# Two decode layers on one core: layer 0's feed-forward in one part, small w2 products in 512 columns, a 24 KB ring and 4 KB more of K kept

## The chip, the cores and the metric

The kernel runs on one core of one Trainium2 chip. The metric is the device time of one execution in microseconds (us); three runs of the kernel before gave 705.28 us in the median, 705.11 at the least and 705.5 at the most. Sizes such as "4 KB" are bytes per partition throughout; a load of 4 KB fills 128 partitions and moves 512 KB.

## What is computed

Two transformer layers, one token for each of four sequences, float32. Both layers use the same weights and the same caches.

```
x = A_x                                      # 4 x 1 x 512
for layer in range(2):
    h = layernorm(x)                         # no gain, no bias
    q = (h @ wq) as 32 heads of 128          # wq 512 x 4096
    p = softmax(q . k_cache / sqrt(128))     # k_cache 4 x 8 x 4096 x 128, four heads share one
    x = x + (p . v_cache) @ wo               # v_cache as k_cache, wo 4096 x 512
    h = layernorm(x)
    x = x + (silu(h @ w1) * (h @ w3)) @ w2   # w1, w3 512 x 1792, w2 1792 x 512
```

The caches hold 64 MiB each and are read once in each layer, apart from what stays on the chip between the layers.

## The kernel before

SBUF is one tile, `arena`, of 218 KB per partition, and the program manages it by hand. A plan (the list `plan`, lines 89 to 160) names every load in order: source, size, the keys under which its parts are used, and, where it matters, a fixed address. `pump` (L164) issues the next loads of the plan on SyncE's queue for as long as `take` (L56) finds room. It is called from `done` (L195) and `vacate` (L203), when the last reader of a load has been issued; the load that takes the room then waits on the chip for those readers. So the order of the loads is fixed, and what paces them is the room.

Each of 8 KV heads has 64 KB of K and 64 KB of V. Scores (L400 to L421) run over 8 blocks of 512 keys, each with four products of 512 columns, one for each sequence, in four column groups of TensorE. Layer 0 takes the heads in rising order, layer 1 in falling order, so that head 7 (`TURN`) is last in the one and first in the other. Between the layers all of wq (64 KB at 0), wo (64 KB at 64) and V of head 7 (64 KB at 128, `KEPT`) stay in `arena`. The first block of head 7's K is partly kept too: layer 0 copies its first 2 KB into PSUM (`keptk`, L417) and the next 2 KB into `first` at the end of `arena` (L418), and layer 1 begins with these (L405 to L408) in place of the first of eight half blocks of 4 KB.

What is left, 28 KB, is the **ring** (L124 to L143): seven slots of 4 KB, six from address 192 on and one at 64, where the first 4 KB of wo lay until they were moved to PSUM (`stash`, L498). Through these slots pass, in the order of the plan, layer 0's w1 and w3 and w2 and then seven half blocks of head 7's K for layer 1. Behind them come blocks 4 to 7 of that K in loads of 8 KB, which take the room that wq's groups leave as layer 1's q products are done (`q_product`, L348).

The feed-forward (L521 to L617) has two parts. The 1792 hidden columns lie as four groups of 448, in four column groups of TensorE; the first part takes 256 of each group's columns, the second the other 192. For layer 0 the pieces are: w1 first part, four of 4 KB; w3 first part, four of 4 KB; w1 second part, four of 3 KB; w3 second part, four of 3 KB; w2, seven of 4 KB, two of its 14 row tiles each. After each piece `busy` (L288) adds products of no use that fill TensorE's time in layer 0. `gate`, `join` and the transposes of the first part run between the products of the second. In layer 1 (not in the ring) the last loads of the program are w1 and w3 of the first part (16 KB each), of the second (12 KB each), and w2 in loads of 8, 8, 4, 4 and 2 KB for row tiles 1 to 13. Row tile 0 of w2 is loaded ahead in another layout (`w2s`): eight tiles of 16 rows in 16 partitions. Each of these and each later row tile is multiplied by `columns` (L554): four products of 128 columns, one for each column group, into `x_ps`. Then 128 columns of `x_ps` are copied and stored.

```
def columns(rows, m, w, last=False):
    for k in range(KC):
        nc.tensor.matmul(x_ps[32 * k:32 * k + B, 0:P], hT[rows, m, :], w[rows, k * P:(k + 1) * P],
                         start=False, stop=last)
```

Of the kernel before, what the change touches and what calls it, by code (L numbers as in the profile page):

```python
# [9 lines left out]
AF = mybir.ActivationFunctionType  # L10
# [13 lines left out]
FA = 2 * P  # L24
FB = FJ - FA
WT = 14
FEW = 16
EPS = 1e-5
SCALE = DH ** -0.5
# [6 lines left out]


@with_exitstack
def tile_decode_layers(ctx: ExitStack, tc: tile.TileContext, x, kt, v, wq, wo, w1, w3, w2, w2s, out):
# [59 lines left out]
    def weights(name, src, layer, parts, per, at=None, first=0):  # L99
        r = 0  # L100
        for n in parts:
            load(src[:, r * KB:(r + n) * KB], per, [(name, layer, first + r // per + j) for j in range(n // per)],
                 None if at is None else at + r)
            r += n

# [10 lines left out]

    def piece(name, i, at):

        w, layer, lo, n, per = {"w1a": (w1, 0, 4 * i, 4, 4), "w3a": (w3, 0, 4 * i, 4, 4),
                                "w1b": (w1, 0, 16 + 3 * i, 3, 3), "w3b": (w3, 0, 16 + 3 * i, 3, 3),  # L120
                                "w2": (w2, 0, 4 * i, 4, 2), "half": (kt[TURN], 1, 4 * i, 4, 4)}[name]
        weights(name, w[:, lo * KB:(lo + n) * KB], layer, (n,), per, at, 2 * i if name == "w2" else i)

    RING = KEPT + 64  # L124
    slots = [WO] + [RING + 4 * i for i in (5, 4, 3, 2, 1, 0)]
    for i in range(4):
        piece("w1a", i, (slots[6], slots[1], slots[2], slots[3])[i])
    for i in range(4):
        piece("w3a", i, (slots[4], slots[5], slots[0], slots[6])[i])
    for i in range(4):  # L130
        piece("w1b", i, RING + 21 - 3 * i)
    for i in range(2):
        piece("w3b", i, RING + 9 - 3 * i)
    piece("w2", 0, slots[0])
    for i in range(2, 4):
        piece("w3b", i, RING + 9 - 3 * i)
    for i in range(1, 7):
        piece("w2", i, slots[i])
    for i in range(7):
        piece("half", i + 1, slots[i])  # L140
    ring["to"] = len(plan) - 1
    cache("k", 1, TURN, (8,) * (NB - SPLIT), SPLIT)
    for n in range(1, HKV):  # L143
# [9 lines left out]
        plan.append((*next(side), "few", None))  # L153

    for part, per, at in (("a", 4, 0), ("b", 3, 16)):
        for name, w in (("w1", w1), ("w3", w3)):
# [7 lines left out]
    def pump():  # L164
        while state["next"] < len(plan):
            src, per, keys, at = plan[state["next"]]
            n = src.shape[-1] // KB
# [12 lines left out]
            if a is None:  # L180
                return
            nc.sync.dma_start(arena[:, a * KB:(a + n) * KB], src)
            i = state["next"]
            if i == 0:
                nc.sync.dma_start(xt[:8], x[:8])
            left[i] = (len(keys), a, n)
            for j, key in enumerate(keys):
                where[key] = (a + j * per, per, i)
            state["next"] += 1

    def loaded(*key):
        a, n, _ = where[key]
        return arena[:, a * KB:(a + n) * KB]

    def done(*key):  # L195
        i = where[key][2]
# [73 lines left out]
    nc.vector.memset(x_ps, 0.0)  # L270

    first = arena[:, FIRST * KB:]
    pT = arena[:, PT * KB:FIRST * KB].rearrange("p (i r) -> p i r", i=NI)

    def small(name, n=1, bufs=1):
# [245 lines left out]
    def feed_forward(layer, mean):  # L521
        keep = layer < LAYERS - 1
        h = p[:, 0:FJ]

        def product(name, ps, lo, n, fill=(0, 0, 0, 0), ks=range(KC)):
            for k in ks:
                w = loaded(name, layer, k)
                for j in range(4):
                    nc.tensor.matmul(ps[32 * j:32 * j + 32, lo:lo + n], x32[:, k, :], w[:, j * n:(j + 1) * n],  # L529
                                     start=(k == 0), stop=(k == KC - 1))  # L530
                done(name, layer, k)
                busy(fill[k] if keep else 0)

        def gate(lo, n):
            a = h[:, lo:lo + n]
# [15 lines left out]
                done("w2", layer, 2 * i + n)  # L551
            busy((1, 2, 2, 2, 1, 2, 0)[i])

        def columns(rows, m, w, last=False):  # L554
            for k in range(KC):
                nc.tensor.matmul(x_ps[32 * k:32 * k + B, 0:P], hT[rows, m, :], w[rows, k * P:(k + 1) * P],  # L556
                                 start=False, stop=last)

        def few(lo, hi):
            for u in range(lo, hi):  # L560
                at = (where["few"] + 2 * u) * KB
                columns(slice(0, FEW), WT + u, arena[:, at:at + 2 * KB])

        sq = squares()
        product("w1a", s_ps, 0, FA, (0, 0, 2, 0))
        rstd = deviation(sq, total(flat(sq)))
        mean()
        if not keep:
            nc.vector.tensor_tensor(xt, xc, mu.unsqueeze(1).broadcast_to([P, KC, B]), op=ALU.add)
        product("w3a", o_ps, 0, FA, (2, 2, 2, 2))  # L570
        if not keep:
            for k in range(KC):
                nc.tensor.matmul(x_ps[32 * k:32 * k + B, 0:P], xt[:, k, :], ident, start=True, stop=False)
            busy(4)
        gate(0, FA)
        join(0, FA)
        product("w1b", s_ps, FA, FB, (1, 1, 1, 1))
        if keep:
            gate(FA, FB)
            nc.scalar.activation(spare, half, AF.Exp)  # L580
        for i in range(2):
            nc.tensor.transpose(t_ps[:, i, :], h[:, i * P:(i + 1) * P], ident)
        if not keep:
            for u in range(8):
                nc.tensor.matmul(t_ps[0:FEW, 2, B * u:B * u + B], h[0:32, FEW * u:FEW * u + FEW], ident[0:32, 0:B],
                                 start=True, stop=True)
            busy()
        tiles(0, 8)
        if not keep:
            nc.vector.tensor_copy(hT[0:FEW, WT:WT + 8, :], t_ps[0:FEW, 2, 0:8 * B].rearrange("p (u b) -> p u b", b=B))  # L590
            gate(FA, FB)
            few(0, 4)
        product("w3b", o_ps, FA, FB, (1, 2, 1, 1), range(0, 2))
        if keep:
            down(0)
        product("w3b", o_ps, FA, FB, (1, 2, 1, 1), range(2, KC))
        join(FA, FB)

        def tail_tiles():
            nc.tensor.transpose(t_ps[:, 2, :], h[:, FA:FA + P], ident)  # L600
            for u in (0, 64):
                nc.tensor.matmul(t_ps[u:u + 64, 3, 0:64], h[u:u + 64, FA + P:FJ], ident[u:u + 64, u:u + 64],
                                 start=True, stop=True)
            tiles(8, 6)

        if keep:
            for i in range(1, WT // 2):
                if i == 4:
                    tail_tiles()
                down(i)  # L610
            return
        few(4, 8)
# [98 lines left out]
```

## Time and profile before

| | before |
|---|---|
| median of 3 runs | 705.28 us |
| the profiled execution | 705.23 us |
| its span, first to last instruction | 703.4 us |
| TensorE matmul busy | 409.9 us (58%) |
| VectorE busy | 85.2 us (12%) |
| ScalarE busy | 38.0 us (5%) |
| GpSimd busy | 3.5 us |
| bytes moved by DMA | 298.85 MB, mean 425 GB/s |
| granted TensorE clock, mean | 0.808 |

The span is what lies between the first and the last instruction; the rest of the profiled execution's time, 1.8 us, lies around it. The DMA share is the mean busy share of the core's 16 DMA engines. It is worked out from the packets' recorded times, so it can go a little above 1 in a short stretch. A granted clock of 1 is 2.4 GHz, and 0.5 is 1.2 GHz.

### The profile page before, as it was taken

To read this page: it belongs to the slowest core of one execution; us is meant where nothing else is said; L and a number is where in the kernel's file an instruction comes from. 1 tells how busy PE (TensorE), PEld (TensorE's weight loads), DVE (VectorE), ACT (ScalarE), POOL (GpSimd) and SP (SyncE) were. 2 spreads that over 40 slices of the span, in tenths; PEclk is the share of its full clock that TensorE was granted. 3 is DMA by queue.
4 is the path that set the end of the run, shared out by engine and by line. 5 is a ranking of instruction groups with operands and counts; after the bars stand their busy time and mean duration, and the time that the engine had idled before them with its cause. 6 is when DMAs were issued, how large, how long until landed. Compare 5 with 4: busy or idle time off the path is not lost. (4 is left out here: it accounts for less than half of the span.)

```text
span 703.4 us, 7079 instructions
## 1 busy us (share of the span) xinstructions
PE 409.9 (58%) x3172; PEld 136.4 (19%) x3172; DVE 85.2 (12%) x291; ACT 38.0 (5%) x87; POOL 3.5 (0%) x11
## 2 busy tenths in 40 slices
PE   2555454456456454538888894365563545467687
PEld 1112011112111111112233331011120111122234
DVE  2001010101001010101111111020000101010111
ACT  0000000000000000101001000000000000000100
POOL 0000000000000000000000000000000000000000
PEclk9986776767777776878999997588787878688899
DMA  9999999999999999999999999999999999999996
GB/s 418 432 403 466 422 418 426 462 415 432 433 444 418 440 444 421 421 428 427 414 404 403 420 431 461 429 425 418 459 425 425 437 444 418 432 433 420 424 424 277
DMA packets 13605, 298.85 MB, mean 425 GB/s; under 512 B 1655, under 2 KB 1783, under 8 KB 6263
## 3 DMA queue, kind: packets, MB, share of 16 engines
q1 hardware_dynamic: 13440, 298.39, 99.1%
q8 instruction: 25, 0.41, 0.2%
q14 instruction: 5, 0.04, 0.0%
q10 hardware_dynamic: 135, 0.01, 0.0%
HBM read 298.33 MB, written 0.07 MB: 424 GB/s over the span
## 5 line engine op out<-in xcount | busy, mean ns | idle before, releaser
L461 PE MATMUL o_ps<-arena 128*32 128x512 f32 x1024 | 146.8, 723 | 144.4 <-DMA arena<-in_v 131.0
L414 PE MATMUL s_ps<-arena,qpad 128*32 128x512 f32 x1020 | 150.1, 742 | 90.1 <-DMA arena<-in_kt 90.1
L461 PEld LDWEIGHTS o_ps<-arena 128*32 128x32 f32 x1024 | 37.4, 130 | 251.9 <-issue 222.4
L414 PEld LDWEIGHTS s_ps<-arena,qpad 128*32 128x32 f32 x1020 | 39.5, 132 | 183.7 <-issue 176.6
L470 DVE SCALAR_TENSOR_TENSOR p<-o_ps,parts,p 128x512 f32<-128x512 f32 x16 | 12.0, 751 | 266.9 <-PE o_ps L461 266.9
L424 DVE TENSOR_REDUCE top<-s_ps 128x1 f32<-128x512 f32 x16 | 11.1, 691 | 196.9 <-PE s_ps L414 196.9
L468 ACT ACTIVATE p<-o_ps,parts 128x512 f32<-128x512 f32 x16 | 11.0, 687 | 189.9 <-PE o_ps L461 182.3
L292 PE MATMUL m_ps<-ident,rows 128*32 128x256 f32 (+1 forms) x84 | 20.9, 352 | 0.0
L352 PE MATMUL o_ps<-arena,xpad 128*32 128x512 f32 x112 | 15.4, 672 | 7.9 <-DMA arena<-in_wq 7.9
L447 PE MATMUL t_ps<-ident,p 128*128 128x128 f32 x64 | 11.4, 305 | 13.5 <-ACT p L441 13.5
L474 PE MATMUL t_ps<-ident,p 128*128 128x128 f32 x64 | 10.5, 287 | 13.9 <-DVE p L470 13.8
L496 PE MATMUL x_ps<-arena,qT 128*4 128x512 f32 x112 | 13.8, 592 | 5.4 <-DVE qT L482 3.6
L434 ACT ACTIVATE f<-d 128x1 f32<-128x1 f32 x16 | 3.2, 203 | 252.8 <-DVE d L432 252.8
L441 ACT ACTIVATE p<-s_ps,top 128x512 f32<-128x512 f32 x16 | 10.9, 684 | 77.3 <-PE t_ps L474 77.3
L448 DVE COPY arena<-t_ps 128x512 f32<-128x512 f32 x16 | 11.1, 691 | 9.7 <-PE t_ps L447 9.7
L474 PEld LDWEIGHTS t_ps<-ident,p 128*128 128x128 f32 x64 | 6.7, 140 | 28.2 <-DVE p L470 28.2
L447 PEld LDWEIGHTS t_ps<-ident,p 128*128 128x128 f32 x64 | 7.3, 150 | 22.2 <-ACT p L441 19.2
L292 PEld LDWEIGHTS m_ps<-ident,rows 128*32 128x32 f32 x84 | 9.0, 110 | 9.0 <-issue 3.5
L529 PE MATMUL o_ps<-arena,xpad 128*32 128x192 f32 (+1 forms) x128 | 8.1, 360 | 1.0 <-DMA arena<-in_w 0.9
L529 PE MATMUL s_ps<-arena,xpad 128*32 128x192 f32 (+1 forms) x128 | 7.9, 359 | 1.3 <-DMA arena<-in_w 1.3
L489 PE MATMUL x_ps<-arena,qT 128*4 128x256 f32 x88 | 6.6, 379 | 2.4 <-DMA arena<-in_w 1.7
L352 PEld LDWEIGHTS o_ps<-arena,xpad 128*32 128x32 f32 x112 | 3.6, 121 | 17.2 <-DMA arena<-in_wq 8.8
(107 smaller groups left out, 144.2 us busy)
## 6 DMA issues: line engine op xcount, KB each, us to landing
arena<-in_v SPq DMA_DIRECT2D x4, 4096.0 KB, 38.4
arena<-in_w SPq DMA_DIRECT2D x17, 512.0 KB, 13.4
arena<-in_kt SPq DMA_DIRECT2D x8, 1024.0 KB, 11.3
arena<-in_kt SPq DMA_DIRECT2D x2, 4096.0 KB, 18.1
arena<-in_wq SPq DMA_DIRECT2D x1, 7168.0 KB, 39.8
arena<-in_v SPq DMA_DIRECT2D x3, 2048.0 KB, 31.8
arena<-in_wo SPq DMA_DIRECT2D x1, 4096.0 KB
arena<-in_kt SPq DMA_DIRECT2D x2, 2048.0 KB
```

The source lines that it names most:

```text
L292: nc.tensor.matmul(m_ps[0:32, (4 - w) * P:], rows, ident.unsqueeze(1).broadcast_to([P, w, P]), start=True, stop=True)
L352: nc.tensor.matmul(ps[32 * k:32 * k + 32, :], xpad[:, 32 * k + lo:32 * k + lo + 32], w[:, k, :], start=first, stop=last)
L414: nc.tensor.matmul(s_ps[32 * b:32 * b + 32, :], qpad[:, 32 * b + lo:32 * b + lo + 32], k[:, j, :], start=(blk == 0), stop=(blk == NB - 1))
L424: nc.vector.tensor_reduce(top[:, 0:1], s_ps, axis=AX.X, op=ALU.max, negate=True)
L447: nc.tensor.transpose(t_ps[:, i, :], p[:, i * P:(i + 1) * P], ident)
L448: nc.vector.tensor_copy(pT.rearrange("p i r -> p (i r)"), t_ps.rearrange("p i r -> p (i r)"))
L461: nc.tensor.matmul(o_ps[32 * b:32 * b + 32, :], pT[:, i, 32 * b:32 * b + 32], w[:, b, :], start=(i == 0), stop=(i == NI - 1))
L468: nc.scalar.activation(p, o_ps, AF.Copy, scale=st["parts"][:, 0:1])
L470: nc.vector.scalar_tensor_tensor(p, o_ps, st["parts"][:, 1:2], p, op0=ALU.mult, op1=ALU.add)
L474: nc.tensor.transpose(t_ps[:, j, :], p[:, j * P:(j + 1) * P], ident)
L496: nc.tensor.matmul(x_ps[r:r + B, :], left(2 * i + n), w(n), start=first, stop=False)
L529: nc.tensor.matmul(ps[32 * j:32 * j + 32, lo:lo + n], x32[:, k, :], w[:, j * n:(j + 1) * n], start=(k == 0), stop=(k == KC - 1))
```

## The change

Layer 0's feed-forward runs in one part: all of w1 in eight pieces of 3.5 KB (one piece is two column groups of 448 columns for one of the four row blocks), then all of w3 in eight such pieces, then `join`, the transposes and w2. The filling products after each piece of w1 and w3 are gone; those after w2's pieces stay, and four units stand behind w3. Layer 1 keeps the two parts (sources `w1l`, `w3l`, laid out as before).

The ring has six slots (24 KB): five from 196 on and the one at 64. The 4 KB at 192 (`MORE`) are kept out of the free room from the start; layer 0 copies the second half of the first block of head 7's K there (GpSimd, 1024 elements), and layer 1 uses it and then gives the room back. So six half blocks are loaded in place of seven.

In layer 1, the eight tiles of 16 rows and row tiles 1 to 4 of w2 are multiplied by `wide`: one product of 512 columns for each, into `s_ps`, four in turn in the four column groups. Then `s_ps` is copied to SBUF and added to `x_ps` by four products of 128 columns. Row tiles 5 to 13 stay with `columns`.

```
+WIDE = 5
+HALF = 2 * FJ / 256
-    PT, FIRST = ARENA - 4, ARENA - 2
-    free = [(WO, PT - WO)]
+    PT, FIRST, MORE = ARENA - 4, ARENA - 2, KEPT + 64
+    free = [(WO, MORE - WO), (MORE + 4, PT - MORE - 4)]
...
-    RING = KEPT + 64
-    slots = [WO] + [RING + 4 * i for i in (5, 4, 3, 2, 1, 0)]
...
-    for i in range(7):
-        piece("half", i + 1, slots[i])
+    RING = MORE + 4
+    slots = [WO] + [RING + 4 * i for i in (4, 3, 2, 1, 0)]
+    small_loads = [(name, i) for name, n in (("w1", 2 * KC), ("w3", 2 * KC), ("w2", WT // 2)) for i in range(n)]
+    small_loads += [("half", i) for i in range(2, 2 * SPLIT)]
+    for n, (name, i) in enumerate(small_loads):
+        piece(name, i, slots[(5, 1, 2, 3, 4, 0)[n % 6]])
...
-                for b, k in enumerate((p, first)):
+                for b, k in enumerate((p, first, more_k[:, 0:BK], more_k[:, BK:])):
...
-                del keys[0]
+                give(MORE, 4)
+                pump()
+                keys = []
...
                 nc.gpsimd.tensor_copy(first, loaded(*keys[0])[:, BK:2 * BK])
+                nc.gpsimd.tensor_copy(more_k, loaded(*keys[0])[:, 2 * BK:])
...
         if keep:
-            for i in range(1, WT // 2):
...
+            product("w1", s_ps)
+            rstd = deviation(sq, total(flat(sq)))
+            mean()
+            gate(0, FJ)
+            nc.scalar.activation(spare, half, AF.Exp)
+            product("w3", o_ps)
+            join(0, FJ)
+            busy(4)
+            for i in range(2):
+                nc.tensor.transpose(t_ps[:, i, :], h[:, i * P:(i + 1) * P], ident)
+            tail_tiles()
+            tiles(0, WT)
+            for i in range(WT // 2):
                 down(i)
             return
...
-            few(0, 4)
...
+        def wide(n, left, w, last=False):
+            r = 32 * (n % 4)
+            nc.tensor.matmul(s_ps[r:r + B, :], left, w, start=(n < 4), stop=last)
+
+        for u in range(8):
+            at = (where["few"] + 2 * u) * KB
+            wide(u, hT[0:FEW, WT + u, :], arena[0:FEW, at:at + 2 * KB])
+            if u == 3:
+                product("w3b", o_ps, FA, FB, range(0, 2))
+        product("w3b", o_ps, FA, FB, range(2, KC))
+        join(FA, FB)
+        busy(2)
         tail_tiles()
-        for m in range(1, WT):
-            columns(slice(0, P), m, loaded("w2", layer, m), m == WT - 1)
+        tiles(8, 6)
+        for m in range(1, WIDE):
+            wide(7 + m, hT[:, m, :], loaded("w2", layer, m), True)
             done("w2", layer, m)
-            if m in (4, 8):
+        nc.vector.tensor_copy(p, s_ps)
+        busy(2)
+        for k in range(KC):
+            nc.tensor.matmul(x_ps[32 * k:32 * k + B, 0:P], rows[:, 0:B], chunk(k), start=False, stop=False)
+        for m in range(WIDE, WT):
+            columns(m, loaded("w2", layer, m), m == WT - 1)
+            done("w2", layer, m)
+            if m == 8:
                 busy(2)
```

## Rows read from the trace of the kernel before

**Rows 1.** The page: DMA's busy share in 40 slices of the span.

```profile
DMA  9999999999999999999999999999999999999996
```

**Rows 2.** The chain of work that ended last, its end (start us, us, what).

```profile
684.32 15.61 DMA arena<-in_w
...
699.97 0.45 PE x_ps L556 x8
```

**Rows 3.** Windows: busy time of each engine, granted clock, DMA share, GB/s.

```profile
247.93:286.76 38.83, 20.72 (x138) 6.12 (x138) 3.44 (x12) 1.67 (x4) 0.00 (x0) 0.69 1.00 431
...
355.00:366.00 11.00, 10.02 (x100) 4.72 (x100) 2.00 (x11) 0.95 (x3) 0.55 (x1) 1.00 1.02 405
```

**Rows 4.** Timeline, PE between the layers: products that waited for loads.

```profile
354.96 0.61 PE L489 MATMUL x_ps<-arena,qT 128*4 128x256 f32 x8 [0.17 <-DMA arena<-in_wo]
...
360.08 0.64 PE L529 MATMUL s_ps<-arena,xpad 128*32 128x256 f32 x8 [0.23 <-DMA arena<-in_w]
...
365.21 0.64 PE L529 MATMUL o_ps<-arena,xpad 128*32 128x256 f32 x8 [0.24 <-DMA arena<-in_w]
...
367.16 0.53 PE L529 MATMUL s_ps<-arena,xpad 128*32 128x192 f32 x8 [0.18 <-DMA arena<-in_w]
...
369.09 0.53 PE L529 MATMUL s_ps<-arena,xpad 128*32 128x192 f32 x8 [0.24 <-DMA arena<-in_w]
...
381.87 0.61 PE L489 MATMUL x_ps<-arena,qT 128*4 128x256 f32 x8 [0.24 <-DMA arena<-in_w]
```

**Rows 5.** Timeline, SyncE's queue: loads issued between the layers (start us, us).

```profile
358.44 1.39 SPq L182 DMA_DIRECT2D arena<-in_w  x3
...
385.78 0.33 SPq L182 DMA_DIRECT2D arena<-in_kt  x1
...
417.61 0.33 SPq L182 DMA_DIRECT2D arena<-in_kt  x1
```

**Rows 6.** The program's first load in the timeline, and a window of half a microsecond.

```profile
0.73 0.38 SPq L182 DMA_DIRECT2D arena<-in_wq  x1
...
1.50:2.00 0.50, 0.00 (x0) 0.00 (x0) 0.47 (x4) 0.50 (x1) 0.00 (x0) 1.00 0.65 115
```

**Rows 7.** Timeline, layer 1's feed-forward from its second part's gate to the end.

```profile
690.26 0.40 DVE L537 SCALAR_TENSOR_TENSOR p<-s_ps,rstd,p 128x192 f32<-128x192 f32 x1
...
690.38 1.05 PE L556 MATMUL x_ps<-arena,qT 16*4 16x128 f32 x32
...
691.37 1.51 PE L529 MATMUL o_ps<-arena,xpad 128*32 128x192 f32 x32
...
694.31 1.06 PE L556 MATMUL x_ps<-arena,qT 128*4 128x128 f32 x32
...
695.18 0.59 PE L292 MATMUL m_ps<-ident,rows 128*32 128x256 f32 x2
...
696.76 1.06 PE L556 MATMUL x_ps<-arena,qT 128*4 128x128 f32 x32 [0.99 <-DMA arena<-in_w]
...
699.30 1.08 PE L556 MATMUL x_ps<-arena,qT 128*4 128x128 f32 x24 [0.63 <-DMA arena<-in_w]
```

**Rows 8.** Timeline: a PSUM copy, products of 512 columns, products of 128.

```profile
328.00 0.69 DVE L448 COPY arena<-t_ps 128x512 f32<-128x512 f32 x1 [0.42 <-PE t_ps L447]
...
344.98 3.62 PE L496 MATMUL x_ps<-arena,qT 128*4 128x512 f32 x32 [1.66 <-DMA arena<-in_wo]
...
686.04 0.40 PE L573 MATMUL x_ps<-ident,xt 128*4 128x128 f32 x8
```

**Rows 9.** Timeline, layer 0's head 7: GpSimd's copy of K, and the next loads.

```profile
294.99 0.61 POOL L418 COPY arena<-arena 128x512 f32<-128x512 f32 x1 [284.45 <-DMA arena<-in_kt]
...
300.58 3.63 SPq L182 DMA_DIRECT2D arena<-in_v  x4
```

**Rows 10.** Windows of 2 us after TensorE fell idle at 303.8 us.

```profile
306.00:308.00 2.00, 0.00 (x0) 0.00 (x0) 0.10 (x1) 0.00 (x0) 0.00 (x0) 1.00 1.14 492
308.00:310.00 2.00, 0.00 (x0) 0.00 (x0) 0.00 (x0) 0.00 (x0) 0.00 (x0) 0.69 1.21 524
```

More of the change, by code (lines that the diff above doesn't have):

```diff
@@ L38, in tile_decode_layers @@
 @with_exitstack
-def tile_decode_layers(ctx: ExitStack, tc: tile.TileContext, x, kt, v, wq, wo, w1, w3, w2, w2s, out):
+def tile_decode_layers(ctx: ExitStack, tc: tile.TileContext, x, kt, v, wq, wo, w1, w3, w1l, w3l, w2, w2s, out):
     nc = tc.nc
@@ L101, in weights @@
         for n in parts:
-            load(src[:, r * KB:(r + n) * KB], per, [(name, layer, first + r // per + j) for j in range(n // per)],
+            load(src[:, int(r * KB):int((r + n) * KB)], per,
+                 [(name, layer, first + r // per + j) for j in range(int(n / per))],
                  None if at is None else at + r)
@@ L117, in piece @@
     def piece(name, i, at):
-        w, layer, lo, n, per = {"w1a": (w1, 0, 4 * i, 4, 4), "w3a": (w3, 0, 4 * i, 4, 4),
-                                "w1b": (w1, 0, 16 + 3 * i, 3, 3), "w3b": (w3, 0, 16 + 3 * i, 3, 3),
+        w, layer, lo, n, per = {"w1": (w1, 0, HALF * i, HALF, HALF), "w3": (w3, 0, HALF * i, HALF, HALF),
                                 "w2": (w2, 0, 4 * i, 4, 2), "half": (kt[TURN], 1, 4 * i, 4, 4)}[name]
-        weights(name, w[:, lo * KB:(lo + n) * KB], layer, (n,), per, at, 2 * i if name == "w2" else i)
-    RING = KEPT + 64
-    slots = [WO] + [RING + 4 * i for i in (5, 4, 3, 2, 1, 0)]
[L126 to L138, printed above, removed]
-    for i in range(7):
-        piece("half", i + 1, slots[i])
+        weights(name, w[:, int(lo * KB):int((lo + n) * KB)], layer, (n,), per, at, 2 * i if name == "w2" else i)
+    RING = MORE + 4
[4 more added lines that the diff above has]
+        piece(name, i, slots[(5, 1, 2, 3, 4, 0)[n % 6]])
     ring["to"] = len(plan) - 1
@@ L192, in loaded @@
         a, n, _ = where[key]
[L193 removed]
+        return arena[:, int(a * KB):int((a + n) * KB)]
     def done(*key):
@@ L523, in feed_forward, with product @@
         h = p[:, 0:FJ]
-        def product(name, ps, lo, n, fill=(0, 0, 0, 0), ks=range(KC)):
+        def product(name, ps, lo=0, n=FJ, ks=range(KC)):
+            parts = 1 if lo or n < FJ else 2
             for k in ks:
[L527 to L532, printed above, removed]
+                for part in range(parts):
+                    w = loaded(name, layer, k * parts + part)
+                    for j in range(4 // parts):
+                        at = 32 * (part * 4 // parts + j)
+                        nc.tensor.matmul(ps[at:at + 32, lo:lo + n], x32[:, k, :], w[:, j * n:(j + 1) * n],
+                                         start=(k == 0), stop=(k == KC - 1))
+                    done(name, layer, k * parts + part)
         def gate(lo, n):
@@ L552, in down, with columns @@
             busy((1, 2, 2, 2, 1, 2, 0)[i])
-        def columns(rows, m, w, last=False):
+        def columns(m, w, last=False):
             for k in range(KC):
-                nc.tensor.matmul(x_ps[32 * k:32 * k + B, 0:P], hT[rows, m, :], w[rows, k * P:(k + 1) * P],
+                nc.tensor.matmul(x_ps[32 * k:32 * k + B, 0:P], hT[:, m, :], w[:, k * P:(k + 1) * P],
                                  start=False, stop=last)
[L559 to L591, printed above, removed]
-            few(0, 4)
[L593 to L597, printed above, removed]
         def tail_tiles():
@@ L610, in feed_forward @@
                 down(i)
             return
-        few(4, 8)
+        product("w1a", s_ps, 0, FA)
+        rstd = deviation(sq, total(flat(sq)))
+        mean()
+        nc.vector.tensor_tensor(xt, xc, mu.unsqueeze(1).broadcast_to([P, KC, B]), op=ALU.add)
+        product("w3a", o_ps, 0, FA)
+        for k in range(KC):
+            nc.tensor.matmul(x_ps[32 * k:32 * k + B, 0:P], xt[:, k, :], ident, start=True, stop=False)
+        busy(4)
+        gate(0, FA)
+        join(0, FA)
+        product("w1b", s_ps, FA, FB)
@@ new lines, in feed_forward @@
+        for i in range(2):
+            nc.tensor.transpose(t_ps[:, i, :], h[:, i * P:(i + 1) * P], ident)
+        for u in range(8):
+            nc.tensor.matmul(t_ps[0:FEW, 2, B * u:B * u + B], h[0:32, FEW * u:FEW * u + FEW], ident[0:32, 0:B],
+                             start=True, stop=True)
+        busy()
+        tiles(0, 8)
+        nc.vector.tensor_copy(hT[0:FEW, WT:WT + 8, :], t_ps[0:FEW, 2, 0:8 * B].rearrange("p (u b) -> p u b", b=B))
+        gate(FA, FB)
+        def wide(n, left, w, last=False):
+            r = 32 * (n % 4)
+            nc.tensor.matmul(s_ps[r:r + B, :], left, w, start=(n < 4), stop=last)
@@ L613, in feed_forward @@
+        for u in range(8):
+            at = (where["few"] + 2 * u) * KB
[5 more added lines that the diff above has]
+        busy(2)
         tail_tiles()
-        for m in range(1, WT):
-            columns(slice(0, P), m, loaded("w2", layer, m), m == WT - 1)
+        tiles(8, 6)
+        for m in range(1, WIDE):
+            wide(7 + m, hT[:, m, :], loaded("w2", layer, m), True)
@@ L616, in feed_forward @@
             done("w2", layer, m)
-            if m in (4, 8):
+        nc.vector.tensor_copy(p, s_ps)
+        busy(2)
+        for k in range(KC):
+            nc.tensor.matmul(x_ps[32 * k:32 * k + B, 0:P], rows[:, 0:B], chunk(k), start=False, stop=False)
[3 more added lines that the diff above has]
+            if m == 8:
                 busy(2)
```

18 lines of the change are left out of this document (10 added, 8 removed).

## The prediction, made before the changed kernel was timed

> **What bounds the kernel now.** I read the DMA line of the page first: at least nine tenths busy in 39 of 40 slices [rows 1]. The end of the chain of waits comes next: what finished last is a load of w2, landed at about 699.9 us, with half a microsecond of TensorE work behind it [rows 2]. So the time is the loads' bytes over their rate, plus a short start and tail, as long as SyncE's queue never runs empty. The windows give the rate: 431 GB/s where loads are 64 KB per partition, 405 in the ring's stage, with DMA's share at 1.00 or more in both [rows 3]. The timeline of that stage shows the ring saturated. TensorE waits for every piece, and four pieces of 4 KB took 365.21 - 360.08 = 5.13 us, 1.28 each; two of 3 KB took 1.93 us, 0.965 each [rows 4]. That is 0.321 us per KB at either size.
>
> **The change, part by part.** All sums are made in the profiled execution (span 703.4 us, its time 705.23 us, 0.05 below the median of 705.28); only differences are used, so they apply to the median as they are.
>
> *One half block of K less.* A load of 4 KB leaves the plan, 512 KB in all. At the ring's pace it is worth 1.28 us [rows 4], at the pace of the large loads 524288 / 431000 = 1.22 us [rows 3]. I take 1.28, since the load stood in the ring; 1.22 is the other end.
>
> *w1 and w3 in pieces of 3.5 KB.* Sixteen loads stay sixteen. Before: 8 x 1.28 + 8 x 0.965 = 18.0 us. After: 16 x 3.5 x 0.321 = 18.0 us. Nothing, while the rate per KB is that of both neighbours in size.
>
> *The smaller ring.* It costs something only if the queue runs empty, so I look for the smallest lead, the time from the issue of a load to the moment when the loads ahead of it are through. What lead is needed shows at the start: the first load was issued at 0.73, and its data moved in the window from 1.5 to 2.0 [rows 6], so at most 1.3 us later. (a) wo's last part is there at 354.96 [rows 4]. The six pieces of w1 behind it end at 354.96 + 6 x 1.12 = 361.7 (seven of 4 KB ended at 363.9). TensorE takes up w1 some 2.8 us behind wo, after the layer norm's sums; the first slot was reloaded at 358.44 [rows 5]. A 3.5 KB piece has two products of 448 columns in two column groups. A product of 512 columns costs 3.62 / 16 = 0.226 us when four groups share the array [rows 8], so a piece takes 4 x 0.226 x 448 / 512 = 0.79 us at most. The reload is issued by about 358.7: 3.0 us of lead where 1.3 are needed. (b) Now `join` and all transposes stand between w3 and w2, with no products to hide them. w3 ends at 354.96 + 18.0 = 372.9. Products 0.79, then what lies between the last w3 product and the tiles' use in layer 1, 691.37 + 1.51 to 694.31 = 1.43 us [rows 7], then 0.61 for the first w2 piece [rows 4]: slot free at 375.8. Its reload is needed at 372.9 + 6 x 1.28 = 380.6. Lead 4.8 us. TensorE catches up with w2 before its last piece, so that is used at 381.87 as before [rows 4]. (c) Layer 1's first norm and q products hang on that moment, so block 4 of K is issued at 385.78 as before [rows 5]. The half blocks ahead of it end at 381.9 + 6 x 1.28 = 389.6, not at 390.9: lead 3.8 us for 5.1. (d) The later loads up to the second of 32 KB, issued at 417.61 [rows 5], have leads above 10 us: 128 KB lie between it and the ring's end, at 38.83 / 128 = 0.303 us per KB [rows 3], 38.8 us. So no lead comes near 1.3, and the 1.28 us pass on to every later landing.
>
> *Copying 4 KB more of K in layer 0.* Two more rows of 512 behind GpSimd's 0.61 us at 294.99 end at about 296.8. Nothing else is queued on GpSimd until the feed-forward, and the load that takes this room is issued at 300.58, when the scores release it [rows 9]. Nothing. In layer 1 the four kept rows replace four products from the ring: the same work.
>
> *Fillers gone.* TensorE waits for loads there either way; nothing on the path, unless the clock falls (below).
>
> *w2's small products in 512 columns.* This lies in the tail, where TensorE had to spare: it waited 0.99 us for row tile 5 and 0.63 for tile 11 [rows 7]. I follow the new order in the times of before (all of it moves up by 1.28). `wide` writes `s_ps`, so it starts behind the gate, at 690.26 + 0.40 = 690.7 and not at 690.38 [rows 7]. Four at 0.226: 691.6. Half of the last w3 products, 1.51 / 2: 692.4. Four `wide`: 693.3. The other half: 694.0. Join and transposes, 1.43: 695.5. Four `wide`: 696.4. The copy of 512 columns, 0.69 [rows 8], and two handovers of 0.05: 697.2. Four products of 128 columns, 0.40 [rows 8]: 697.6. Tiles 5 to 8, 1.06: 698.6. The filler 0.59: 699.2 [rows 7]. Tiles 9 and 10, 0.53: 699.7. Tile 11 is there at 699.30. Busy times count each group's drain, which the next one overlaps by some 0.2 us, about five times, so the true arrival is nearer 698.8. Late by 0.4 at worst, then 0.8 us for three tiles: 700.5 against 700.42 before. Cost 0 to 0.1 us; I take 0, since the array's overlap shows in the rows that I added up. `wide` saves nothing at the end either, because loads set it.
>
> **Sum:** -1.28 us: 705.28 - 1.28 = **704.0 us**, 0.18% less. About 0.2% (1.4 us) is what a measurement of this kernel can tell from no change, so this lies just inside.
>
> **The rivals.**
>
> *R1, room paces the loads.* If a lead falls short, DMA idles and the gain is given back there, up to all of it: 704.0 to 705.3, say 704.7. Places: the seventh piece (margin 1.7 us) and K's block 4 (margin 2.5). What could do it is a slow TensorE. For: the fillers are gone, so TensorE works 0.79 of each 1.12 us, where it was busy 10.02 of 11 us at a granted clock of 1.00 [rows 3]. Against: the gaps are of 0.3 us, and in a true pause, idle from 303.8 on, the clock was still 1.00 from 306 to 308 and fell only after that [rows 10]. The Trainium skill (TensorE: Matmul & The Clock Gate, Part 1) says that the throttled state is the default and activity releases it; that speaks against taking fillers away, and by it the halved clock would make step (b) 2.8 us longer and leave 2 us of its lead.
>
> *R2, slower.* The place is the eight products with 16 rows in the contraction. If these don't run side by side in four column groups, each takes 0.90 in place of 0.226: 8 x 0.68 = 5.4 us more on TensorE's path in the tail, of which 0.5 at most is spare. 704.0 + 4.9 = 709. It decides from 3.3 us of extra on: 0.5 are spare, and 2.8 separate 704.0 from slower by 0.2%. Against: the 128-row products in the same four groups do share the array [rows 8], and the 16-row ones of 128 columns took 1.05 us for 32, as the 128-row ones took 1.06 [rows 7].
>
> *R3, each load costs a fixed time.* Then one load less is worth more than its bytes: with the 1.3 us of the start unhidden, 705.28 - 1.28 - 1.3 = 702.7. Against: 4 and 3 KB differ by 0.318 us, which leaves a fixed part of 0.01 us per queued load [rows 4]. The Trainium skill (DMA: Bandwidth & Descriptors, Anatomy of one DMA) fits transfers on GpSimd's path as 2.0 us plus the bytes; by that fit the time would be near 702.0, and the trace of these queued loads disagrees.
>
> *R4, the change doesn't save what it says.* If rows of 3.5 KB moved 7% worse per KB than those of 3 and 4, 18.0 x 0.07 = 1.26 us would be gone: 705.3. No row shows that size.
>
> **How the numbers follow.** Forecast 0.73, R1 0.13, R2 0.06, R3 0.03, R4 0.05. The forecast's own spread is about 0.3 us either way: 0.06 from the two rates, 0.1 from the tail, 0.2 from runs that lie 0.4 us apart (705.11 to 705.5). The bound of 0.2% lies at 703.87, 0.13 below 704.0, so 0.4 of the forecast's chance is faster by more. Faster: 0.73 x 0.4 + 0.03 = 0.32. Slower: R2, 0.06. Same: 0.62. The range runs from 703.4 to 705.1: the forecast with its spread and most of R1. It leaves out R2, R3, R4's half and the edges, about 0.15.
>
> **What would show it.** Right: six loads of 512 KB from K in the ring; pieces of w1 and w3 landing every 1.12 us; K's first waits after 440 us ended 1.3 us sooner; DMA still at nine tenths in each slice; in the tail TensorE waiting for tile 11 and for tile 13. Wrong: the DMA share falling between 355 and 391 (R1), a granted clock under 1 there, 16-row products of 512 columns at 0.9 us each (R2), or TensorE without a wait before tile 11, which would put the tail on TensorE's path.

## The result, and the profile after

The changed kernel takes 708.2 us in the median of 15 runs, the kernel before 705.23 in 15 runs: 1.0031 times as long, 95% interval 1.0022 to 1.0041. Ratios here and below weigh all of the runs; the two medians alone would give 1.0042. Each experiment was timed beside the kernel before, and they ran on three chips. It is slower by 0.3%, and outside the range. Its executions also lie far apart, from 704.83 to 709.16 us: four below 706, eleven from 707.0 up. Those of before lie between 705.0 and 705.53. The profiled execution took 708.26 us, so it is one of the eleven.

| | before | after |
|---|---|---|
| median | 705.23 us | 708.2 us |
| profiled execution, span | 705.23, 703.4 us | 708.26, 706.4 us |
| bytes moved, mean rate | 298.85 MB, 425 GB/s | 298.31 MB, 422 GB/s |
| granted TensorE clock, mean | 0.808 | 0.809 |

The page of the changed kernel, its DMA lines (busy tenths in 40 slices; packets and bytes):

```profile
DMA  9999999999999999999999999999999999999995
...
DMA packets 13460, 298.31 MB, mean 422 GB/s; under 512 B 1639, under 2 KB 1767, under 8 KB 6119
```

The bytes fell by 0.54 MB, and the load that is gone holds 0.52. The slices answer to [rows 1] and hide what matters: a slice is 17.7 us long, and a hole of 2 us in it still reads 9. The end of the chain of waits, which answers to [rows 2] (start us, us, what):

```profile
688.08 1.51 PE s_ps L528 x32
...
692.20 0.86 PE o_ps L528 x16
693.05 1.81 PE s_ps L604 x8
694.87 1.44 PE o_ps L528 x16
696.30 0.83 PE m_ps L285 x2
...
697.95 1.86 PE s_ps L604 x8
699.84 0.70 DVE p L619
700.58 0.40 PE x_ps L622 x8
```

Before, this chain ended in a load. Now it is TensorE with short copies between, from 688.08 to the end of its work at 703.43, without one load in it: the forecast's own sign of being wrong, TensorE without a wait before tile 11. The windows of the tail (busy time of PE, PEld, DVE, ACT, POOL, then granted clock, DMA share, GB/s) say why:

```profile
691.00:692.00 1.00, 0.87 (x8) 0.10 (x8) 0.08 (x1) 0.00 (x0) 0.00 (x0) 1.00 0.99 414
692.00:693.00 1.00, 0.97 (x23) 0.43 (x21) 0.00 (x0) 0.00 (x0) 0.00 (x0) 1.00 0.99 410
693.00:694.00 1.00, 1.00 (x12) 0.09 (x8) 0.00 (x0) 0.00 (x0) 0.00 (x0) 0.52 1.07 442
...
698.00:699.00 1.00, 1.00 (x8) 0.17 (x1) 0.18 (x1) 0.00 (x0) 0.00 (x0) 0.50 0.46 178
699.00:700.00 1.00, 1.00 (x6) 0.17 (x1) 0.16 (x1) 0.00 (x0) 0.00 (x0) 0.57 0.10 37
700.00:702.00 2.00, 1.72 (x50) 1.27 (x49) 0.53 (x1) 0.00 (x0) 0.00 (x0) 1.00 0.01 4
```

From 693 to about 699.9 the granted clock is at the lower level, 0.5. TensorE was 0.87 and 0.97 busy in the two microseconds ahead of the fall. The timeline shows what the level does (start us, us, engine, line, tile, shapes):

```profile
691.13 1.04 PE L604 MATMUL s_ps<-arena,qT 16*4 16x512 f32 x8 [0.36 <-DVE p L535]
692.20 0.86 PE L528 MATMUL o_ps<-arena,xpad 128*32 128x192 f32 x16
692.98 1.88 PE L604 MATMUL s_ps<-arena,qT 16*4 16x512 f32 x8
694.80 1.51 PE L528 MATMUL o_ps<-arena,xpad 128*32 128x192 f32 x16
...
697.88 1.89 PE L604 MATMUL s_ps<-arena,qT 128*4 128x512 f32 x8
```

The same group of four `wide` products took 1.04 us and then 1.88; the same half of w3, 0.86 and then 1.51. The last two loads landed at 699.64 and 700.28 (from semaphore records), and TensorE came to their tiles after 702. The second place is the ring. Its windows, in the stage behind wo and ahead of K's block 4:

```profile
355.00:366.00 11.00, 9.71 (x62) 3.60 (x60) 1.28 (x8) 0.48 (x2) 0.00 (x0) 1.00 0.89 330
358.00:359.00 1.00, 1.00 (x12) 0.46 (x13) 0.35 (x2) 0.00 (x0) 0.00 (x0) 1.00 0.64 255
359.00:360.00 1.00, 1.00 (x12) 0.26 (x6) 0.00 (x0) 0.00 (x0) 0.00 (x0) 1.00 0.36 140
360.00:361.00 1.00, 0.82 (x10) 0.14 (x4) 0.00 (x0) 0.00 (x0) 0.00 (x0) 1.00 0.75 118
361.00:362.00 1.00, 0.76 (x6) 0.14 (x4) 0.00 (x0) 0.00 (x0) 0.00 (x0) 1.00 0.90 301
...
389.00:391.00 2.00, 2.00 (x24) 1.12 (x16) 0.26 (x2) 0.40 (x1) 0.00 (x0) 1.00 0.99 360
```

In 355 to 366 the loads moved 330 GB/s where they had moved 405 [rows 3]: the queue ran dry for some 2 us. SyncE's queue and TensorE's products there, which answer to [rows 5] and [rows 4]:

```profile
358.41 1.99 PE L528 MATMUL s_ps<-arena,xpad 128*32 128x448 f32 x16
...
359.40 1.75 SPq L174 DMA_DIRECT2D arena<-in_w  x4
...
367.62 0.95 PE L528 MATMUL o_ps<-arena,xpad 128*32 128x448 f32 x4 [0.18 <-DMA arena<-in_w]
368.75 0.95 PE L528 MATMUL o_ps<-arena,xpad 128*32 128x448 f32 x4 [0.19 <-DMA arena<-in_w]
369.88 0.94 PE L528 MATMUL o_ps<-arena,xpad 128*32 128x448 f32 x4 [0.18 <-DMA arena<-in_w]
...
383.50 0.61 PE L485 MATMUL x_ps<-arena,qT 128*4 128x256 f32 x8 [0.24 <-DMA arena<-in_w]
387.41 0.33 SPq L174 DMA_DIRECT2D arena<-in_kt  x1
```

The first slot was reloaded at 359.40 (forecast 358.7), with TensorE at w1 at 358.41, 0.7 us later than before; in this execution the granted clock was 0.59 in the mean from 345 to 349, where wo is multiplied; in the kernel before it was 1.00. Once the queue ran again, pieces of 3.5 KB came every 1.13 us, as forecast. The last piece of w2 was used at 383.50 and K's block 4 issued at 387.41, each 1.6 us later than before; the forecast was no later.

So there are two theories to test. **Tail:** the halved clock puts TensorE on the path; rival: 16-row products share the array badly (R2). **Ring:** the smaller ring runs dry and gives the saved 1.28 us back (R1); rivals: the bytes were never worth 1.28 us, or the one-part form costs.

### The profile page after: what moved, and what is told of

Same layout as the page of the kernel before. It is cut to its first block, busy times and chain, and to the rows that moved or that the text cites. A ratio compares the mean times of both kernels' runs of the same rounds, so it can differ in the third digit from the quotient of the medians.

```text
span 706.4 us, 6783 instructions
## 1 busy us (share of the span) xinstructions
PE 410.9 (58%) x3024; PEld 131.6 (19%) x3024; DVE 85.4 (12%) x289; ACT 37.7 (5%) x86; POOL 4.5 (1%) x12
## 2 busy tenths in 40 slices
DMA packets 13460, 298.31 MB, mean 422 GB/s; under 512 B 1639, under 2 KB 1767, under 8 KB 6119
## 5 line engine op out<-in xcount | busy, mean ns | idle before, releaser
L409 PE MATMUL s_ps<-arena,qpad 128*32 128x512 f32 x1016 | 147.1, 736 | 88.8 <-DMA arena<-in_kt 88.8
L492 PE MATMUL x_ps<-arena,qT 128*4 128x512 f32 x112 | 16.1, 654 | 6.1 <-DVE qT L478 3.6
L285 PE MATMUL m_ps<-ident,rows 128*32 128x256 f32 (+1 forms) x64 | 16.9, 378 | 0.0
L528 PE MATMUL o_ps<-arena,xpad 128*32 128x448 f32 (+2 forms) x96 | 11.3, 454 | 1.1 <-DMA arena<-in_w 1.1
L528 PE MATMUL s_ps<-arena,xpad 128*32 128x448 f32 (+2 forms) x96 | 9.2, 420 | 1.4 <-DMA arena<-in_w 1.0
L285 PEld LDWEIGHTS m_ps<-ident,rows 128*32 128x32 f32 x64 | 7.0, 114 | 9.2 <-issue 4.9
```

The lines of the kernel that those rows point to most:

```text
L285: nc.tensor.matmul(m_ps[0:32, (4 - w) * P:], rows, ident.unsqueeze(1).broadcast_to([P, w, P]), start=True, stop=True)
L492: nc.tensor.matmul(x_ps[r:r + B, :], left(2 * i + n), w(n), start=first, stop=False)
L528: nc.tensor.matmul(ps[at:at + 32, lo:lo + n], x32[:, k, :], w[:, j * n:(j + 1) * n], start=(k == 0), stop=(k == KC - 1))
```

## The experiments

**The ring alone.** The changed kernel with the tail of before.

```
-        for u in range(8):
-            wide(u, hT[0:FEW, WT + u, :], arena[0:FEW, at:at + 2 * KB])
+        few(0, 4)
...
-        for m in range(1, WIDE):
-            wide(7 + m, hT[:, m, :], loaded("w2", layer, m), True)
+        for m in range(1, WT):
+            columns(m, loaded("w2", layer, m), m == WT - 1)
```

> The changed kernel with the tail of before (all small products through columns). Theory, two separate losses (the ring runs dry behind wo and gives back the 1.28 us; the 512-column products let TensorE's clock fall in the tail): DMA's share falls under 0.8 between 358 and 361, the granted clock stays 1.00 after 674, and the time is 704.8 to 705.6 with little spread between runs. Rival A, all of the loss is in the tail and the dip is made up later: 704.0. Rival B, all of the loss is in the ring: 707 to 708.

Measured: 705.39 us in the median of 11 (704.59 to 706.47), 1.0004 times before, interval 0.9995 to 1.0012. The saved load brings nothing. I had expected little spread and a clock of 1.00 from 674 on; both missed. Its first reload behind wo, the stage around it and the tail:

```profile
358.69 2.03 SPq L174 DMA_DIRECT2D arena<-in_w  x4
```

```profile
354.00:362.00 8.00, 7.50 (x54) 2.69 (x48) 0.94 (x5) 0.47 (x2) 0.00 (x0) 1.00 0.93 340
358.00:359.00 1.00, 1.00 (x12) 0.23 (x4) 0.00 (x0) 0.00 (x0) 0.00 (x0) 1.00 0.66 262
...
691.00:692.00 1.00, 0.56 (x20) 0.25 (x12) 0.00 (x0) 0.00 (x0) 0.00 (x0) 0.95 1.04 434
692.00:693.00 1.00, 1.00 (x16) 0.65 (x12) 0.00 (x0) 0.00 (x0) 0.00 (x0) 0.50 0.97 401
...
695.00:696.00 1.00, 1.00 (x29) 0.59 (x21) 0.03 (x1) 0.00 (x0) 0.00 (x0) 0.84 0.95 371
```

The hole behind wo is there again, though here the first slot was reloaded at 358.69, just as forecast: a late TensorE is not what makes it. The clock fell in this tail too, for 3.4 us, and TensorE waited for none of the last loads. But these landed at 699.90 (before 699.93) and TensorE ended 0.5 us later, as it did before: the tail of before had just that much to spare.

**The wide tail alone.** The kernel before with the changed kernel's tail of layer 1.

```
-            few(0, 4)
+        for u in range(8):
+            wide(u, hT[0:FEW, WT + u, :], arena[0:FEW, at:at + 2 * KB])
...
+        for m in range(1, WIDE):
+            wide(7 + m, hT[:, m, :], loaded("w2", layer, m), True)
```

> The kernel before with the changed tail only (wide products, copy, four products). Theory of two losses and rival A: the granted clock falls to 0.5 in most executions some 3 us after the first wide product, TensorE ends last, 707 to 709 in the median with executions spread from 705.3 upward. Rival B: 705.3, with TensorE waiting for tile 11.

Measured: 707.66 us in the median of 5 (707.5 to 707.9), ratio 1.0033, interval 1.0021 to 1.0045: this part alone loses as much as the whole change. The clock was at 0.5 from 692.6 to 699.4, and the same groups as in the changed kernel grew:

```profile
690.91 1.04 PE L594 MATMUL s_ps<-arena,qT 16*4 16x512 f32 x8 [0.36 <-DVE p L537]
...
692.67 1.89 PE L594 MATMUL s_ps<-arena,qT 16*4 16x512 f32 x8
```

**One load left out**, the ring as before: half block 1 isn't loaded.

```
-    for i in range(7):
+    for i in range(1, 7):
         piece("half", i + 1, slots[i])
...
-                for b, k in enumerate((p, first)):
+                for b, k in enumerate((p, first, p, first)):
```

> The kernel before without the load of one half block of layer 1's K: the first block's scores of two sequences use the kept columns of the other two in its place, so that part of the scores is changed. It prices the load by itself, with the ring and everything else as before. If bytes set the time: 704.0, 1.2 to 1.3 less than before. If room paced the loads: 705.3. If each load cost a fixed time too: 702.7.

Measured: 704.99 us in the median of 12 (704.33 to 706.61, and one of 713.38), ratio 1.0007, interval 0.9988 to 1.0026. Most of the 1.28 us is missing even with seven slots. The profiled execution is the one of 713.38 us, at a granted clock of 0.679 in the mean, so the profile to read is that of the same kernel's repetition, below.

**One part with 28 KB.** Layer 0's feed-forward as changed, with seven slots and seven half blocks and the tail of before.

```
-    PT, FIRST, MORE = ARENA - 4, ARENA - 2, KEPT + 64
-    free = [(WO, MORE - WO), (MORE + 4, PT - MORE - 4)]
+    PT, FIRST = ARENA - 4, ARENA - 2
+    free = [(WO, PT - WO)]
```

> The kernel before with layer 0's feed-forward in one part only: pieces of 3.5 KB through seven slots, seven half blocks of K, tail of before. Theory: 24.5 KB are ahead when wo ends, 3.5 more than in the changed kernel, so the dip of DMA's share comes about 1 us later or not at all, 705.2 to 705.8. If the one-part form itself costs the time (fillers, later transposes): 706 or more. If it is the ring's size alone: 705.3 and no dip.

Measured: 704.95 us in the median of 11 (704.52 to 705.42), ratio 0.9995, interval 0.9987 to 1.0004, below all that I had named. The one-part form costs nothing in the time. Its windows still show a short hole behind wo (374 GB/s from 354 to 362; before 407), and its clock was at 0.5 in the tail from 691.8 to 695.2.

**Bytes taken from a large load.** The kernel before, K of head 2 in layer 0 without its last 4 KB.

```
+        if (which, layer, g) == ("k", 0, 2):
+            load(src[:, 0:60 * KB], 8, [(which, layer, g, j) for j in range(NB)])
+            return
```

> The kernel before with 4 KB less in one large load (K of layer 0's third head is loaded without its last 4 KB, so the scores of two of its sequences' last block use what lay there; that part is changed). It prices 512 KB where the next load is issued more than 10 us ahead, so no engine can run dry. If bytes set the time: 1.2 us less, 704.0. If the gain is lost even there: 705.2.

Measured: 704.08 us in the median of 11 (703.88 to 704.19), ratio 0.9983, interval 0.9974 to 0.9992. So 512 KB are worth 1.14 us where the queue is never dry.

**Only the 16-row tiles wide, and only the 128-row tiles wide.** The two halves of the wide tail, each edit shown against the wide tail alone; the second takes row tiles 1 to 8 in place of 1 to 4.

```
-            wide(7 + m, hT[:, m, :], loaded("w2", layer, m), True)
+            columns(slice(0, P), m, loaded("w2", layer, m))
```

> The kernel before with the eight 16-row tiles in 512 columns, copy and four products, and row tiles 1 to 13 through columns. If the 16-row products of 512 columns let the clock fall: 707 to 708, clock 0.5 for some 7 us from about 692, as with the whole changed tail. If the 128-row ones do: 705.3.

```
-        for u in range(8):
-            wide(u, hT[0:FEW, WT + u, :], arena[0:FEW, at:at + 2 * KB])
+        few(0, 4)
...
+        few(4, 8)
+        for m in range(1, 9):
+            wide(m - 1, hT[:, m, :], loaded("w2", layer, m), m > 4)
```

> The kernel before with the 16-row tiles through columns and row tiles 1 to 8 in 512 columns, copy and four products. If the 16-row products are the cause: 705.2 to 705.6, with the clock back to 1.00 by 696 at the latest. If the 128-row ones or the copy are: 707 to 708.

Measured: 16-row tiles 705.54 us (ratio 1.0011, interval 1.0002 to 1.002), in two groups: seven of 11 runs from 705.10 to 705.54, four from 707.09 to 707.16, nothing between. 128-row tiles 705.21 us (0.9999, interval 0.999 to 1.0008), all within 704.99 to 705.46. The first kernel's timeline:

```profile
690.67 1.04 PE L594 MATMUL s_ps<-arena,qT 16*4 16x512 f32 x8 [0.36 <-DVE p L537]
...
692.43 1.04 PE L594 MATMUL s_ps<-arena,qT 16*4 16x512 f32 x8
```

In this execution the clock stayed at 1.00, and both groups took 1.04 us. Up to here TensorE's work is that of the wide tail alone, whose second group took 1.89. So the work ahead of it doesn't settle whether the clock falls, and the gap of 1.6 us between the two groups of times is what a fall would make. No profile shows one of the four, so that last step is argued. The wide tail was timed on another chip than its halves, so a difference between chips is a rival that no run here excludes.

**Two parts with a 24 KB ring.** The kernel before with 4 KB more of K kept and six slots of 4 KB, its pieces of 3 KB in these slots too.

```
-    PT, FIRST = ARENA - 4, ARENA - 2
+    PT, FIRST, MORE = ARENA - 4, ARENA - 2, KEPT + 64
...
-    slots = [WO] + [RING + 4 * i for i in (5, 4, 3, 2, 1, 0)]
+    slots = [WO] + [RING + 4 * i for i in (4, 3, 2, 1, 0)]
...
+        piece(name, i, slots[(5, 1, 2, 3, 4, 0)[n % 6]])
```

> The kernel before with 4 KB more of K kept and the ring of six slots, the feed-forward in two parts (pieces of 4 and 3 KB) and the tail as before. 24 KB are ahead when wo ends, not 21, so the dry stretch comes about 1 us later and is shorter. Theory of engines that run dry at their own times: DMA's share dips less than in the ring-alone kernel, 704.1 to 705.0. If what the smaller ring costs does not depend on the bytes ahead: 705.4, as the ring alone.

Measured: 706.31 us in the median of 11 (705.22 to 707.17), ratio 1.0016, interval 1.0008 to 1.0025. I had expected 704.1 to 705.0, so this missed. Its profiled execution, the fastest of the 11, behind wo and in the stage after:

```profile
354.00:362.00 8.00, 7.36 (x75) 3.73 (x78) 1.34 (x9) 0.47 (x2) 0.21 (x1) 1.00 0.99 384
362.00:380.00 18.00, 14.71 (x167) 6.26 (x159) 2.04 (x7) 2.38 (x4) 0.35 (x1) 1.00 1.02 385
```

A piece of 3 KB in a slot of 4 KB leaves six such slots with 18 KB under way, and the rate falls from 401 to 385 GB/s over 18 us. This looks like the same fault in another place, made by my packing.

**Fillers in the tail.** The changed kernel with the clock held up, if fillers do that.

```
-        busy()
+        busy(3)
         tiles(0, 8)
...
             if u == 3:
+                busy(2)
                 product("w3b", o_ps, FA, FB, range(0, 2))
+        busy(2)
```

> The changed kernel with fillers in layer 1's tail: the one unit ahead of the hidden values' copy becomes three, and two units each stand behind the first four and behind the last four products of 16 rows. Theory (the granted clock halves TensorE in the tail, and does so because TensorE runs thin there): the fillers keep the clock at 1.00 through 690 to 700 us; they lengthen TensorE's path by about 2 x 0.59 = 1.2 us, less what waits for loads anyway, so 705.2 to 706.2 us in every execution, none over 707. Rival A (the fall comes whatever stands beside these products): the clock at 0.5 again for some 7 us in most executions, the fillers at twice their time, 709 to 711. Rival B (the clock is not what costs, TensorE's path is too long by itself): clock at 1.00 and still 708 or more.

Measured: 706.12 us in the median of 11 (705.49 to 706.66), ratio 1.0013, interval 1.0004 to 1.0022. Work was added to the engine that sets the end, and the median is 2.1 us below the changed kernel's (1.3 by the ratios, since four runs of the changed kernel were fast). The window and the timeline of its tail:

```profile
693.00:694.00 1.00, 1.00 (x18) 0.21 (x9) 0.00 (x0) 0.00 (x0) 0.00 (x0) 1.00 1.02 410
...
698.00:699.00 1.00, 0.60 (x18) 0.38 (x20) 0.56 (x1) 0.00 (x0) 0.00 (x0) 1.00 0.30 115
```

```profile
691.28 1.04 PE L604 MATMUL s_ps<-arena,qT 16*4 16x512 f32 x8
...
693.45 1.04 PE L604 MATMUL s_ps<-arena,qT 16*4 16x512 f32 x8
...
696.76 1.04 PE L604 MATMUL s_ps<-arena,qT 128*4 128x512 f32 x8
...
698.84 1.06 PE L554 MATMUL x_ps<-arena,qT 128*4 128x128 f32 x32
```

The clock is 1.00 throughout, 16-row and 128-row groups take the same 1.04 us, and no run reaches 707, though five of 11 lie above the 706.2 that I had set. The end is TensorE's even so, with no load in its last chain. That a halved clock costs the time stands; that it fell because TensorE ran thin is not shown, since the fillers ran on one more chip and one execution was profiled. R2's account, that 16-row products don't share the array, falls.

**A 24 KB ring with nothing more kept.** The ring alone, but with seven half blocks loaded and the 4 KB beside the ring unused.

```
-    small_loads += [("half", i) for i in range(2, 2 * SPLIT)]
+    small_loads += [("half", i) for i in range(1, 2 * SPLIT)]
```

> One-part feed-forward and a ring of six slots, as in the changed kernel, but seven half blocks are loaded as before and the 4 KB beside the ring stay unused; tail as before. It splits the loss of the changed ring into (a), the stage behind wo, and (c), K's block 4. Theory (both places lose, because 4 KB that hold K are 4 KB that hold no load on its way): the DMA share dips at 358 to 362 us as in the run of the ring alone and not at 387 to 391; 704.95 of the one-part kernel with seven slots plus about 0.7, so 705.5 to 705.9 us, and the run of the ring alone (705.39) then gave back another 0.8 to 1.1 us at K's block 4. Rival (all of the loss is at the stage behind wo): 705.39 + 1.28 = 706.7 us.

Measured: 712.02 us in the median of 4, ratio 1.0096, interval 1.0082 to 1.011. It can't split the loss as I had meant. A seventh half block has no slot of its own among six: it waits in SyncE's queue until layer 1 has used half block 1, and block 4 stands behind it. SyncE waited 8.1 us for that product, and DMA stood still:

```profile
389.00:391.00 2.00, 2.00 (x18) 1.15 (x18) 0.17 (x1) 0.59 (x1) 0.00 (x0) 1.00 0.04 14
391.00:395.00 4.00, 4.00 (x38) 1.34 (x42) 0.16 (x1) 0.00 (x0) 0.00 (x0) 1.00 0.37 91
```

So in this plan a 24 KB ring needs the K kept. What the next kernel shows is block 4 by itself.

**One load left out, again,** for a profile (the same kernel, the same diff).

> The kernel before without the load of half block 1 (columns kept already are used a second time in its place, so part of the scores is not the reference's), once more, for a profile of it. Theory (with 24 KB in place of 28 ahead of K's block 4, the queue runs dry there): no dip of the DMA share at 358 to 362 us, a dip of 0.7 to 1.1 us in sum between 386 and 392, time near 704.8. Rival (the bytes are simply worth less): no dip anywhere, time near 704.8. Rival (the load is worth its 1.28 us): no dip, 704.0.

Measured: 704.61 us in one run. Its windows behind wo and around K's block 4:

```profile
354.00:362.00 8.00, 7.33 (x78) 3.67 (x71) 1.44 (x9) 0.47 (x2) 0.45 (x1) 1.00 1.03 409
...
380.00:400.00 20.00, 19.77 (x178) 8.18 (x182) 2.61 (x14) 1.81 (x5) 0.55 (x1) 1.00 1.00 400
```

No hole behind wo (409 GB/s; before 407), but 400 GB/s in 380 to 400 where before moved 416: 16 x 20 / 405 = 0.8 us lost ahead of block 4. I had expected 0.7 to 1.1 us of it between 386 and 392; there it is 0.6 (377 GB/s for 416). Even with seven slots, a load less leaves 24 KB ahead of block 4, and here that is too little.

**2 KB kept, a ring of 26 KB**, one part, pieces of 3.5 KB close together, seven of them: meant to beat both.

```
+    spots = [RING, RING + 18.5, RING + 15, RING + 11.5, RING + 8, RING + 4.5, WO]
+    for n, (name, i) in enumerate([(name, i) for name in ("w1", "w3") for i in range(2 * KC)]):
+        piece(name, i, spots[n % 7])
...
+    load(kt[TURN][:, 6 * KB:8 * KB], 2, [("half", 1, 1)], RING)
```

> A version meant to be faster than both: one-part feed-forward in layer 0, 2 KB more of K kept in place of 4 (so half block 1 is a load of 2 KB), a ring of 26 KB in which the pieces of 3.5 KB stand close together, seven of them, tail of the kernel before. Theory (bytes save 0.32 us per KB, and the lead of seven pieces is that of the one-part kernel with 28 KB): 704.95 - 0.64 = 704.3 us, up to 704.6 if the fastest engines still run dry ahead of K's block 4. Rival (each KB kept is lost again as lead): 704.95 us.

Measured: 705.25 us in the median of 11 (704.82 to 706.68), ratio 1.0003, interval 0.9994 to 1.0012. The rival was the nearer one (704.95): what is kept is lost as lead. No kernel here that computes everything beats the one before by more than the intervals.

**The ring's account.** Bytes that didn't move, from the windows of each profile, as time at 405 GB/s against before (407, 401 and 416 GB/s in the three stretches). For the ring alone in the first: (407 - 340) x 8 / 405 = 1.3 us.

| kernel | queued behind wo | 354 to 362 | 362 to 380 | 380 to 400 | saved by bytes |
|---|---|---|---|---|---|
| before | 7 x 1.28 = 9.0 us | 0 | 0 | 0 | 0 |
| one load left out, again | 9.0 us | 0.0 | -0.2 | 0.8 | 1.28 |
| one part, 28 KB | 7 x 1.12 = 7.8 us | 0.7 | -0.2 | 0.0 | 0 |
| 2 KB kept, 26 KB | 7.8 us | 0.6 | 0.0 | 0.4 | 0.64 |
| two parts, 24 KB | 6 x 1.28 = 7.7 us | 0.5 | 0.7 | 0.0 | 1.28 |
| ring alone, 24 KB | 6 x 1.12 = 6.7 us | 1.3 | -0.3 | 0.5 | 1.28 |
| changed kernel | 6.7 us, TensorE 0.7 us later | 2.1 | -0.2 | 0.2 | 1.28 |

The hole behind wo grows as the queue shortens. Losses less savings give the load left out -0.7 us and its profiled execution stood at -0.6; two parts -0.1 and 0.0; the ring alone +0.3 and +0.1. One part (+0.4 against 0.0) and 2 KB kept (+0.4 against +1.2, one of the slowest of its runs) agree less well. Each row rests on one profiled execution; that of two parts is its fastest run, 1.1 us under its median, and the account doesn't explain the slower ones.

## Why the prediction was wrong

By medians, the ring alone stands at +0.2 us where -1.3 was forecast, and the wide tail alone at +2.4 where 0 was; together 2.6 of the 3.0 us by which the changed kernel is slower. The changed kernel's later start at w1, with a deeper hole behind wo, is a likely part of the rest, which no run separates.

**The bound** was right for the loads: their bytes set the time where the queue is full, and 512 KB are worth 1.14 us (forecast 1.22 to 1.28). **Pieces of 3.5 KB** cost nothing, at 1.13 us each, and R4 is out. R3 has nothing for it: no kernel with a load less or shorter gained more than its bytes.

**The smaller ring failed in step (a)**, "3.0 us of lead where 1.3 are needed". The reload came when forecast in the ring alone (358.69), and the queue ran dry all the same. The lead ran to 361.7, the landing of the last of six queued pieces, and a landing is complete when the last of 16 DMA engines is through. The trace counts the landings one engine at a time (us, worked out from semaphore records):

| one load's landings | first engine | median | last |
|---|---|---|---|
| wo's last part, before | 351.49 | 353.0 | 354.92 |
| sixth piece of w1, ring alone | 358.35 | 359.73 | 361.57 |
| sixth piece of w1, changed kernel | 358.38 | 359.67 | 361.71 |

The median engine is some 2 us ahead of the landing that TensorE waits for, the first more than 3 us. So 3.0 us of lead is about 1 us for half of the engines and less than none for the first, with 1.3 needed. Seven pieces of 4 KB, 2.2 us more, cover it: before, there is no hole (407 GB/s). The Trainium skill (DMA: Bandwidth & Descriptors, Why a DMA increments its semaphore by 16 and not by 1) says that the up to 16 engines of one DMA finish independently and that only the full count means that all has landed; the spread of 3.4 us agrees. The forecast read a queue's end from landings and forgot the 15 other ends.

A second fault comes on top: an engine's landing counts some time after its data has moved. At 360.0 in the changed kernel two engines were still moving data (worked out from packet records), and seven of the sixth piece's 16 landings were to come. The needed 1.3 us run from an issue to the first data, so the lead should have ended at the data too. How much of the hole this makes, beside the spread, is open.

**Step (c) failed** in the same way. I gave it 3.8 us of lead; the load left out loses 0.8 us there with everything else as before. In the changed kernel itself this place cost less, 0.2 us by the account, and the place behind wo 2.1. In the changed kernel w2's last piece was also not "used at 381.87 as before" but at 383.50, because the hole behind wo had delayed it. Step (b) held in the changed kernel: no loss from 362 to 380. So R1, given 0.13, is what happened in the ring, at both places that it named, and in the ring alone it took all of the 1.28 us. Its "slow TensorE" was not needed: through the ring's stage the granted clock was 1.00. A fall ahead of that stage came with the later w1 and a hole of 2.1 us in place of the ring alone's 1.3.

**The tail** was summed with durations at a granted clock of 1.00, and there the sum is about right. From the first `wide` group to tiles 5 to 8 it allowed 697.6 - 690.7 = 6.9 us. With fillers that took 698.84 - 691.28 = 7.6 us, and the two fillers in it that the sum hasn't are 0.59 us each at most, so 6.4 us or a little more without them. The step that failed is the condition: the clock fell in the profiled execution, and by the times in most others, and the groups from 693 on grew by 0.84, 0.65, 0.47, 0.3 and 0.85, in all 3.1 us. TensorE's path had 0.5 us to spare at most by the forecast's own figure; the wide tail alone, whose groups grew as much, lost 2.4 us. I had named a fall of the clock as a danger for the ring and not for the tail. The Trainium skill (TensorE: Matmul & The Clock Gate, Part 1) takes the throttled state as the default that activity releases; the kernel with fillers agrees in its one profiled execution, with 1.00 where the changed kernel had 0.5.

**R2** named the place, the time (709) and the sign, and its mechanism is refuted: the 16-row products do run side by side, 1.04 us for four as for 128 rows at a clock of 1.00, and 1.88 against 1.89 at 0.5.

## What to carry over

Count a queue's lead from its first and median DMA engine, not from the landing that a consumer sees; and where the queue is as long as the chain it has to cover, room given to kept data is lead taken from loads, so a saved load saves nothing. Before putting fewer and wider products into a tail, ask what it costs at the lower clock, and price it by rows at 0.5 as well as at 1.00. Test a part under suspicion by itself, and on the same chip: here each of two parts was harmless or nearly so in most runs and the pair was not, but the pair ran on another chip.

## What was not expected of the hardware

- The granted clock fell to 0.5 beside a TensorE that was 0.87 to 1.00 busy (0.56 in the microsecond ahead of the fall in the ring alone), and, by the times of the 16-row kernel in two groups 1.6 us apart, in some executions of one program and not in others. With fillers of 128 rows it was 1.00 in the profiled execution, and no run stood apart. What decides a fall was not settled.
- Kernels whose ring ran dry spread over 1.9 us from run to run (704.59 to 706.47, 705.22 to 707.17, 704.82 to 706.68); the kernel before and the one with the short large load, whose rings didn't, over 0.5 in its 15 runs and 0.3. But one part with 28 KB, whose ring ran dry for 0.7 us, spread over 0.9 alone. The cause is open; a fall of the clock in the tail in some runs is one candidate.
